# Batch 0's values as ten half loads, with a new order of all steps, in an attention and mixing kernel

## The chip, the cores and the metric

The kernel runs on one core of one Trainium2 chip. The metric is the device time of one execution in microseconds (us). The core's engines are named as in the profile: PE (TensorE, the matrix products; PEld is its weight load), DVE (VectorE), ACT (ScalarE), POOL (GpSimd) and SP (SyncE, which here issues all DMAs). Each engine executes its own instructions in order.

## The reference

Batch 8, 8 heads, 576 positions, head size 64. For each batch and head two attentions are added:

```
out_up    = repeat4( softmax(scale * q_d k_d^T) v_d )           # q_d, k_d, v_d: means of 4 positions
out_local = softmax(scale * q k^T where |i - j| < 4) v          # a band of 7 positions
x = out_up + out_local                                          # then to (8, 576, 512)
theta = x @ w_theta
y = w_tok_r @ (x * cos(theta)) + w_tok_i @ (x * sin(theta))     # over the 576 positions
u = x + y
out = u + max(u @ w_ch, 0)
```

All inputs and the output are float32; the products run in bfloat16.

## The kernel before, in words

**The work of a batch.** It is cut into small steps, each a Python function that issues a few instructions, and each named by two letters. A number behind the letters, as in mx 0.3, is the batch and the part.

- Loads: `lk` and `lq` bring k and q, one load of 288 KB for each pair of heads, four of each in a batch. `lv` and `lw` bring v in ten half loads of 128 KB, two for each of five chunks of positions. All land in 14 float32 buffers `st`.
- `ck`, `cq`, `cv` cast these to bfloat16, on DVE (v), ACT (a) or POOL (g). `tp` turns k and q on PE (nine 128x128 turns), `ev` evicts them into kT and qT. `kd` and `qd` form the sums of four positions.
- Local attention: `ps` (scores of one of three units), `ex` (exp on ACT), `mk` (mask, on DVE or POOL), `po` (product with v, five chunks), `nm` (normalise, two DVE instructions).
- Attention of the means: `pv` and `vd` (means of v), `sd` (scores), `ed` (exp), `nd` (product), `xn` (normalise), `xd` and `xc` (turn and evict).
- `xt` turns the local part and `xa` adds both into xT. Then `th` (theta), `cs` (cos and sin on ACT), `xm` (turn x back), `zz` (x times cos and sin, into z). The last 64 positions go through `tt`, `ct`, `zt` and, in batches 0 to 3, `zp` and `zc`; in batches 4 to 7 a transposing DMA, `dz`.
- Mixing over positions: `mx`, eight groups of nine products a batch (line 610), each evicted by `ua` (line 615). Then `up` and `uc` (turn), `ch` (product with w_ch), `rl` (max and add), `st` (store). The last 64 positions of two batches go together through `ht` and `rt`.

**Weights.** `la`/`ca` bring w_theta, `lc`/`cc` bring w_ch. `lb` loads w_tok_r and w_tok_i in nine pieces, `cb` casts them, `wp` turns them on PE and `wc` evicts them into WT. The first `mx` needs all of WT and all of batch 0's z.

**What sets the order.** `ORDER` is a string of some 1,200 words, one a step: two letters, and then the engine, the PSUM bank or the `st` buffer. The steps are issued in exactly that order, and the function `pin` chains all instructions of an engine, so each engine's order is the string's. `wm` issues products of a zero tile (line 715) that nothing reads: place and count, `wm0k` is 20 of them. `te` and `ts` load ACT's table for exp and for sin (line 720).

**Batch 0's v.** For the batches in `VT` v comes in another way than by `lv` and `lw`: `l1` loads it like k and q (four loads of 288 KB), `c1` casts, `t1` turns on PE, `e1` evicts on ACT, and `x1` turns it again into the five chunks, from where `cv` evicts it into v_w.

Of the kernel before, what the change touches and what calls it, by code (L numbers as in the profile page):

```python
# [55 lines left out]
l10 l11 c1g c1g k0 l12 lk3 l14 ckg c1v lk5 wm0k t101 c1g e1a kcg wm24 t123 e1a lq6 wm45 x12 cva ckg x13 cva x10 cvv
cqg lq7 lk8 lk9 tp45 cqg kcg kcg x12 lqa eva lqb kdg cvv kca cka wm62 tp67 lkc x13 lkd cvv eva ckv wm13 pv01 cqv lq0
la2 cqg lb1 tp45 qdv eva wm22 tp23 eva wm65 ps67 kdg vdv lq3 qdv ckg cka ps45 cag ex wm25 sd23 ex lb4 ed cbg lk5 sd01  # L60
cqg ps67 mkv ed po45 nm po23 nd45 nd01 la6 nm la7 xn xn lk8 mkg tp23 cag po45 ex xt6 po01 cqa eva la9 lqa mkg caa xd7
lqb ckg xca ckg nm tp23 nm xt4 xt5 lbd cag lbc cbg lb2 xt7 xa cqg lb1 eva lb0 cbg lb3 lb6 tp01 xa po23 th4 xa xm5 xa
lv7 cqg nm cbg th6 lw xt7 cbg th2 lv5 xm3 evv cbg ts cs tp01 lv8 lv9 cs cbg xa tt4 zz cs xm5 wp6 wp2 zz lw lw wp3 lw
lv4 lw cbg lqa zz ct lqd eva qdg ztv wp7 cba th4 wcv zp5 lkb xm6 wcv lkc kdg wcv wp2 wp3 wcv zcv wp0 wcv wp1 cs wp7
wca wcv ps45 lk2 lk1 wcv wcv ps23 te ex qdg ps01 lq0 zz kdv cva ex mx7 mx6 mx4 cvg ua sd23 cvg cvg mkv lc3 ex po01 ua
sd67 ed ed mkv mx5 ua nm po23 ua po01 cvg pv67 nm nm mkg vda mx4 ua po23 lq6 cqg po67 nd01 nm nd45 mx2 up3 xn lq7 ckg
xn cqg lk5 cka nm tp01 xd4 lk8 up5 uca eva xcv xt3 ucv lk9 tp67 cka xt4 xt0 ua ckg xt1 kdg lv4 xa xa xa mx5 xa eva lva
tp23 ua th4 xt0 lw xa evv cqg th5 xm1 lvb lcd lqc tt0 lw lk1 lv2 lv0 lw ts cs lw xm4 cqg cs tp67 ckg cqg th2 xm3 th5
ct lw cka zz tp01 cs qdg zz cs xm2 evv ztg lc6 lc5 zp4 mx6 ccg zz qdg zcv zz eva cvg mx7 ps45 te ex ua ps23 ua ckg kdv
ex mkv ps01 mx6 lq7 mx7 po45 sd23 ex lq8 lk3 kdg ed cvg sd01 cqg ckg ua lk4 lq9 mx6 tp23 mkv lva lw lvc lw nm ua tp45  # L70
up7 cvg mkv cvv ed mx0 eva cvg pv23 ccg ua ucv eva po67 po45 ua nm up1 nm vda ccg ccg ch0 nd67 lq1 xn nd23 lkb cqg cqa
tp45 uca qdg xn mx1 xd2 xt3 eva ps67 rl lq0 ua po45 xcv kdg qdg ps01 ch2 xa ckg ex mkg nm rl mx3 ps67 cqg lv2 cka po45
ex ua sd01 lkd xt2 ckg ex nm mx3 xt4 xt5 xa up2 ua cqa cqg tp67 cvv ed up3 xa evv uca th0 xa lv6 xt1 up2 xa lw th4 xm6
ucv ts cs uca th5 cvg lq5 ckg po01 cvg zz cs nm po23 xm7 cs ch6 nm tt4 tp01 lw ct tp23 th5 rl mkg ch4 lq7 zz st eva
evv rl po67 sd01 cs cqg cvg ztg po23 ch5 nm nm rl ch4 lv8 lw te ed cvg st pv67 vda zp0 zca lk4 cka lk3 lk1 tp23 cqa
mkg ckg lq9 lqb rl qdg lva lw xm1 eva ckg utg lv0 zz lw xm5 ch4 nd67 lvc zz xn lw nd01 mx5 lvd xn mx6 st ps23 rl lv2
# [25 lines left out]
def kernel(  # L102
# [290 lines left out]
    def cv(b, c, w):  # L393
        if b in VT:
            COPY[w](out=v_w[b % 2][:, c, :, 0:D], in_=at.pop(("x1", b, c)).rearrange("p (h d) -> p h d", d=D))
            return
        COPY[w](out=v_w[b % 2][:, c, :, 0:D], in_=at["v", b, c].rearrange("p (h d) -> p h d", d=D))  # L397
# [360 lines left out]
```

## Time and profile before

| | us |
|---|---|
| median of 3 runs | 236.6 (235.68 to 238.39) |
| the profiled execution | 236.41 |
| its span, first to last instruction | 234.7 |
| PE busy | 223.5 (95%) |
| DVE busy | 187.6 (80%) |
| ACT busy | 159.7 (68%) |
| POOL busy | 143.9 (61%) |

The span lies inside the execution's own time, 1.7 us less. An engine's busy time counts its computing instructions alone. PE's busy time includes the products of the zero tile, and PE's matrix products overlap one another, so a busy PE is not PE at its peak.

### The profile page before, as it was taken

The numbers are of one execution on the slowest core, as the hardware profiler recorded it, in microseconds if no ns is written. First come the engines' busy times: TensorE is split into PE (matmuls) and PEld (weight loads), VectorE is DVE, ScalarE is ACT, GpSimd is POOL, SyncE is SP. The second block draws the span as 40 slices with busy tenths as digits, with TensorE's granted clock in tenths as the row PEclk, the third lists the DMA queues.
The fourth block names the chain that finished last, engine by engine and source line by source line (L and its number), as shares of the span: only waits on it lengthen the run. The fifth ranks groups of instructions, "written<-read, shape, count | busy, mean of one in ns | idle before, by whom it ended". The sixth has DMA issues, their size and how long they took to land.

```text
span 234.7 us, 8524 instructions
## 1 busy us (share of the span) xinstructions
PE 223.5 (95%) x3500; PEld 155.7 (66%) x3500; DVE 187.6 (80%) x377; ACT 159.7 (68%) x239; POOL 143.9 (61%) x190
## 2 busy tenths in 40 slices
PE   7998899999999699999999999899999999999992
PEld 3555767687787466786688757676676665577740
DVE  5169997999898689888799869969898879466472
ACT  2389898669987779869987796859889358510000
POOL 7858999809999995983874628794598310100000
PEclk9999999999999999999999999999999999999998
DMA  6999979996959999999986206996967357674477
GB/s 196 383 392 386 287 163 276 391 244 143 290 162 250 243 345 212 224 224 244 287 183 173 61 0 141 292 236 139 127 155 169 73 124 197 91 221 109 110 226 244
DMA packets 76647, 49.35 MB, mean 210 GB/s; under 512 B 61120, under 2 KB 61120, under 8 KB 76608
## 3 DMA queue, kind: packets, MB, share of 16 engines
q1 hardware_dynamic: 76608, 48.81, 81.4%
q8 instruction: 27, 0.44, 0.8%
q14 instruction: 12, 0.10, 0.2%
HBM read 33.98 MB, written 9.44 MB: 185 GB/s over the span
## 4 chain that ended last, share of the span: by engine, by line
PE 85%; DVE 8%; issue 3%; DMA 2%; ACT 1%; SPq 0%; DVEq 0%
PE PS L610 29%; PE PS L635 12%; PE PS L548 10%; PE PS L304 5%; PE PS L531 3%; PE PS L512 3%; PE PS L715 3%; PE PS L587 2%; PE PS L483 2%; DMA z<-zT 2%; PE PS L275 2%; DVE tmp L521 2%; PE PS L448 2%; PE PS L624 2%; PE PS L652 1%
## 5 line engine op out<-in xcount | busy, mean ns | idle before, releaser
L610 PE MATMUL PS<-WT,z 128*128 128x288 bf16 x576 | 77.9, 286 | 0.4 <-DMA z<-zT 0.4
L610 PEld LDWEIGHTS <-z 128*128 128x128 bf16 x576 | 54.3, 98 | 16.0 <-DMA z<-zT 0.7
L615 DVE TENSOR_TENSOR uT<-PS,xT 128x288 bf16<-128x288 f32 x64 | 28.8, 452 | 12.4 <-PE PS L610 11.9
L548 PE MATMUL PS<-wth,xT 128*128 128x512 bf16 x128 | 32.2, 379 | 0.0
L635 PE MATMUL PS<-wch,uT 128*128 128x512 bf16 x128 | 31.1, 379 | 0.0
L569 POOL TENSOR_TENSOR zT<-xT,cst 128x512 bf16<-128x512 bf16 x7 | 8.1, 1153 | 35.9 <-ACT cst L566 27.6
L521 DVE TENSOR_TENSOR tmp<-PS,rl 128x512 bf16<-128x512 f32 x40 | 27.6, 691 | 1.4
L502 POOL TENSOR_TENSOR pm<-pm,band 128x1024 bf16<-128x1024 bf16 (+1 forms) x14 | 25.1, 1792 | 5.5 <-ACT pm L491 5.5
L537 DVE TENSOR_TENSOR xT<-PS,xdT 128x464 bf16<-128x464 f32 (+1 forms) x40 | 24.0, 628 | 4.5 <-PE PS L531 2.3
L640 DVE SCALAR_TENSOR_TENSOR osb<-PS,ur 128x512 f32<-128x512 f32 x32 | 21.8, 684 | 5.2 <-PE PS L635 4.9
L491 ACT ACTIVATE pm<-PS 128x1024 bf16<-128x1024 f32 (+1 forms) x24 | 20.4, 880 | 6.4 <-PE PS L483 6.4
L553 ACT ACTIVATE cs<-PS,pihc 128x512 bf16<-128x512 f32 x32 | 22.1, 692 | 3.0 <-PE PS L548 2.8
L331 POOL TENSOR_TENSOR two<-kT 128x580 f32<-128x580 bf16 x13 | 15.0, 1154 | 9.4 <-ACT kT L317 6.6
L720 ACT ACT_TABLE_LOAD x15 | 19.2, 1283 | 0.3
L635 PEld LDWEIGHTS <-uT 128*128 128x128 bf16 x128 | 11.9, 98 | 11.1
L554 ACT ACTIVATE cs<-PS 128x512 bf16<-128x512 f32 x32 | 19.2, 600 | 0.0
L594 DVE TENSOR_TENSOR z<-PS,cs 128x1024 bf16<-128x1024 bf16 x24 | 16.0, 681 | 2.4 <-PE PS L587 2.1
L548 PEld LDWEIGHTS <-xT 128*128 128x128 bf16 x128 | 11.2, 98 | 9.8 <-DVE xT L537 0.4
L438 ACT ACTIVATE pd<-PS 128x864 bf16<-128x864 f32 x16 | 13.8, 888 | 5.6 <-PE PS L427 5.6
L331 POOL TENSOR_TENSOR two<-qT 128x576 f32<-128x576 bf16 x13 | 14.9, 1148 | 4.3 <-ACT qT L317 4.0
L397 POOL CAST v_w<-st 128x512 bf16<-128x512 f32 x26 | 16.2, 647 | 0.0
L531 PE MATMUL PS<-ident,tmp 128*128 128x116 bf16 (+1 forms) x160 | 13.9, 215 | 2.1 <-issue 2.0
(116 smaller groups left out, 435.8 us busy)
## 6 DMA issues: line engine op xcount, KB each, us to landing
st<-in_k_dram SPq DMA_DIRECT2D x32, 288.0 KB, 5.3
st<-in_q_dram SPq DMA_DIRECT2D x32, 288.0 KB, 5.9
st<-in_v_dram SPq DMA_DIRECT2D x70, 128.0 KB, 5.0
out_dram<-osb SPq DMA_DIRECT2D x32, 256.0 KB, 3.0
st<-in_v_dram SPq DMA_DIRECT2D x4, 288.0 KB, 3.4
st<-in_moe_w_tok_r_dram SPq DMA_DIRECT2D x4, 288.0 KB, 6.3
st<-in_moe_w_tok_i_dram SPq DMA_DIRECT2D x4, 288.0 KB, 6.1
st<-in_moe_w_theta_dram SPq DMA_DIRECT2D x4, 256.0 KB, 7.2
```

What stands on the lines that cost most here:

```text
L331: nc.gpsimd.tensor_tensor(out=t, in0=src[:, :, 0:2], in1=src[:, :, 2:4], op=ALU.add)
L491: nc.scalar.activation(out=pm[(3 * b + u) % NPM][:, :, 0:n].rearrange("p e c j w -> p e (c j w)"), in_=at.pop(("ps", b, u))[:, :, 0:4 * W ...
L502: EW[w].tensor_tensor(out=t, in0=t, in1=m, op=ALU.mult)
L521: nc.vector.tensor_tensor(out=tmp[(NCH * b + c) % NTMP].rearrange("p g (j d) -> p g j d", d=D), in0=ps[:, :, :, 0:D], in1=r.unsqueeze(3).t ...
L531: nc.tensor.matmul(out=ps[:, kk::2, STEP * g:STEP * g + OWN[n]], lhsT=t[:, g, P * kk:P * kk + P], rhs=identw[:, :, lo:lo + OWN[n]], start= ...
L537: nc.vector.tensor_tensor(out=xT[b % 2][:, :, CH * c:CH * c + cnt].rearrange("p e (m j) -> p e m j", j=4), in0=at.pop(("xt", b, c))[:, :, ...
L548: nc.tensor.matmul(out=ps, lhsT=xT[b % 2][:, dc, P * c:P * c + P], rhs=wth[:, dc, :], start=(dc == 0), stop=(dc == 3))
L553: nc.scalar.activation(out=t[:, 0, :], in_=ps, func=AF.Sin, bias=pihc, scale=1.0)
L610: nc.tensor.matmul(out=ps, lhsT=z[b % 2][:, j, P * dc:P * dc + P], rhs=WT[:, j, cols], start=(j == 0), stop=(j == 8))
L615: nc.vector.tensor_tensor(out=uT[b % 2][:, dc, cols], in0=at.pop(("mx", b, i)), in1=xT[b % 2][:, dc, cols], op=ALU.add)
L635: nc.tensor.matmul(out=ps, lhsT=uT[b % 2][:, dc, P * c:P * c + P], rhs=wch[:, dc, :], start=(dc == 0), stop=(dc == 3))
L640: nc.vector.scalar_tensor_tensor(out=o, in0=at.pop(("ch", b, c)), scalar=0.0, in1=ur[b % 2][:, c, :], op0=ALU.max, op1=ALU.add)
```

## The change

`VT` is empty, so batch 0's v comes by `lv` and `lw` like that of the other batches; `l1`, `c1`, `t1`, `e1` and `x1` issue nothing. All words of `ORDER` are new in their order, and in many the engine, bank or buffer is another. No function is changed.

```
-VT = (0,)
+VT = ()
...
 ORDER = """
-l10 l11 c1g c1g k0 l12 lk3 l14 ckg c1v lk5 wm0k t101 c1g e1a kcg wm24 t123 e1a lq6 wm45 x12 cva ckg x13 cva x10 cvv
...
+lq0 lk1 lk2 lq3 cka ckv lq4 cqg wm0m tp01 cqv lk5 lk6 k0 wm24 tp23 ckv eva lq7 cqv lv8 lv9 lw ckv cqg lw lva lw lvb
...
 """
```

Of the zero-tile products there were 46 in eight places, now 67 in eleven. `te` and `ts` stood 15 times, now 17.

**SP at the start of the program.** Before, its first eight loads are v (line 367), k and q (line 288) of batch 0:

```order
L367 DMA st0_127<-in_v_dram 128x576
L367 DMA st1_128<-in_v_dram 128x576
L367 DMA st2_129<-in_v_dram 128x576
L288 DMA st3_130<-in_k_dram 128x576
L367 DMA st4_131<-in_v_dram 128x576
L288 DMA st5_132<-in_k_dram 128x576
L288 DMA st6_133<-in_q_dram 128x576
L288 DMA st7_134<-in_q_dram 128x576
```

In the changed kernel the first eight are all of batch 0's q and k. From the eighth on it reads:

```order
L288 DMA st7_134<-in_q_dram 128x576
L349 DMA st8_135<-in_v_dram 64x8x64
L349 DMA st9_136<-in_v_dram 64x8x64
L349 DMA st8_135<-in_v_dram 64x8x64
L349 DMA st9_136<-in_v_dram 64x8x64
L349 DMA st10_137<-in_v_dram 64x8x64 x2
L349 DMA st11_138<-in_v_dram 64x8x64 x2
L349 DMA st12_139<-in_v_dram 64x8x64
L288 DMA st13_140<-in_k_dram 128x576
L349 DMA st12_139<-in_v_dram 64x8x64
L288 DMA st1_128<-in_k_dram 128x576
L259 DMA st0_127<-in_moe_w_tok_r_dram 128x576
```

The v loads moved from the front of the queue behind batch 0's k and q, and are ten (line 349) where they were four.

**DVE between batch 0's last addition into xT and the first mixing.** Before, line 537 is `xa` 0.4, line 594 `zz`, line 569 `zt`, line 279 `wc`, line 582 `zc`:

```order
L537 TENSOR_TENSOR xT0_101<-PS_61,xdT0_99 128x4x112
L594 TENSOR_TENSOR z0_103<-PS_61,cs0_105 128x1024
L594 TENSOR_TENSOR z0_103<-PS_61,cs1_106 128x1024
L594 TENSOR_TENSOR z0_103<-PS_61,cs2_107 128x1024
L569 TENSOR_TENSOR zT_111<-xT0_101,cst_109 128x512
L279 COPY WT_126<-PS_61 128x576 x4
L582 COPY z0_103<-PS_61 128x512
L279 COPY WT_126<-PS_61 128x576 x4
L594 TENSOR_TENSOR z0_103<-PS_61,cs3_108 128x1024
```

And in the changed kernel, with line 323 a `kd` of batch 1:

```order
L537 TENSOR_TENSOR xT0_101<-PS_61,xdT0_99 128x4x112
L279 COPY WT_126<-PS_61 128x576
L323 TENSOR_REDUCE kd1_67<-kT1_63 128x2x5x29
L279 COPY WT_126<-PS_61 128x576
L594 TENSOR_TENSOR z0_103<-PS_61,cs0_105 128x1024
L569 TENSOR_TENSOR zT_111<-xT0_101,cst_109 128x512
L594 TENSOR_TENSOR z0_103<-PS_61,cs1_106 128x1024
L279 COPY WT_126<-PS_61 128x576 x5
L594 TENSOR_TENSOR z0_103<-PS_61,cs2_107 128x1024
L594 TENSOR_TENSOR z0_103<-PS_61,cs3_108 128x1024
```

One `kd` came in ahead of the products into z, and `zc` left DVE for ACT.

**ACT in the thetas of batches 4 and 5.** Lines 553 and 554 are cos and sin of one chunk, 565 and 566 those of the last 64 positions. Before, batch 5's first pairs have an eviction and the last positions between them:

```order
L720 ACT_TABLE_LOAD
L720 ACTIVATE idle_143<-pihc_142 128x1
L553 ACTIVATE cs0_105<-PS_61,pihc_142 128x512
L554 ACTIVATE cs0_105<-PS_61 128x512
L314 COPY qT1_65<-st11_138 128x1152
L553 ACTIVATE cs1_106<-PS_61,pihc_142 128x512
L554 ACTIVATE cs1_106<-PS_61 128x512
L565 ACTIVATE cst_109<-PS_61,pihc_142 128x4x64
L566 ACTIVATE cst_109<-PS_61 128x4x64
```

In the changed kernel the last of batch 4 and all four of batch 5 follow one another, behind a table load that comes after the exp of batch 6:

```order
L720 ACT_TABLE_LOAD
L720 ACTIVATE idle_143<-pihc_142 128x1
L553 ACTIVATE cs3_108<-PS_61,pihc_142 128x512
L554 ACTIVATE cs3_108<-PS_61 128x512
L553 ACTIVATE cs0_105<-PS_61,pihc_142 128x512
L554 ACTIVATE cs0_105<-PS_61 128x512
L553 ACTIVATE cs1_106<-PS_61,pihc_142 128x512
L554 ACTIVATE cs1_106<-PS_61 128x512
L553 ACTIVATE cs2_107<-PS_61,pihc_142 128x512
L554 ACTIVATE cs2_107<-PS_61 128x512
L553 ACTIVATE cs3_108<-PS_61,pihc_142 128x512
L554 ACTIVATE cs3_108<-PS_61 128x512
```

Five pairs of cos and sin now stand in a row on ACT at this place, where there were single ones.

More of the change, by code (lines that the diff above doesn't have):

```diff
@@ L51 @@
 QKD = (7,)
-VT = (0,)
+VT = ()
 ORDER = """
[L58 to L76, printed above, removed]
@@ new lines @@
+kdv wp3 tt1 th2 cbg wcv eva cbg ct wp6 wp1 zz xm4 ztv zz wcv lq7 lq2 lv4 lv8 cs xm3 wca lv9 wm53 wp7 cs lkb lw cqg zp5
+cqg zca cka wcv lka lqc wp4 lw qdg wcv wp0 wcv wp2 wp1 wcv xm5 wca tp67 eva zz lvd zz kdg tp01 eva lw mx4 ckg lv0 mx5
+ps23 ua lw mx4 lw ps67 lk5 lk1 ua te ex lq6 qdv mkg ua sd01 sd23 cvg cqa lq3 mx5 ed mx4 cvv ex ua ua cka po01 po67 ed
+nm cqa lv7 lkb wm51 ps45 tp23 ex nm lc2 lc8 lc4 mkg cvv cvg lca lkc lw lqd lv9 tp01 cvg eva ckg eva ckg up4 ucv mx5
+up4 mkv pv67 vda ua lq0 lw po23 cqg cqg lv5 nm po01 lw mx5 nm uca nd23 tp67 nd01 ua eva xn tp45 po23 xt6 kdg eva xn nm
@@ new lines @@
+xt7 ccg xd0 lk1 qdg ccg xca xt1 xa ps45 ps23 lv6 xa xa cka ckg mx0 xt6 ex ex lv3 ccv kdg ccv ua xt7 cvg xa th4 ts cs
+th5 cs up1 xm0 tp23 lw xa th6 th7 mkv lq2 lkb evv zz tt4 ch5 lq4 cs mkv xm0 lw lk8 zz rl xm6 lqa cs cqg ct lvc lk7 cqg
+tp23 xm7 zz ucv up0 ch4 qdg uca ch5 ztg zz eva rl zp6 ckg zcv cvg lvd cvg rl cqg mx7 lq0 sd01 lw po23 cvg nm te ed
+ps45 ua ex mx6 lq1 po01 sd23 ckg ua kdg cqa nm po45 mx7 ed tp01 lw nm mx6 po23 ua cvv pv45 eva tp01 mkg qdg ua lk9 mx7
+vda ckg nm kdv eva cqa cka lq5 ua nd23 nd45 lk2 mx0 cqa ps67 qdg xn lv6 ex xn ckg ua po23 ps45 lw utg lvb lv4 lw nm
@@ new lines @@
+cva ex ckg mkv ch1 cvg cqg rl sd67 ed xd0 mx2 sd45 ed xcv po01 xt3 ua cqa up2 lw nm ucv st tp67 up4 cvg lq3 cvg lk8
+tp01 mx2 lva eva cvg xt5 ucv xa tp67 eva xt3 ua lv7 xa xa xt2 tp01 eva up4 xt3 up5 kdg lk0 xa lw ucv po67 ucv eva lkc
+xm2 xa nm ps45 qdv ps01 ex tt3 pv45 mkv cqg ch6 rl ex th7 vda nd01 ts ct nd45 lv9 xn xn ckg cs ztg th6 lw cs th3 mkv
+po01 po45 ch7 lk2 kdg lw lqd xd6 zz nm th2 xm0 st rl ckg cs xca lq1 lq5 cqg nm xt1 xt3 zz xa lk6 zp7 tp45 cs xm6 zz xa
+xt2 zca eva xm0 lkb ch1 zz po67 nm ps45 te ex mx3 xa xt0 lv4 lw th6 xt2 lq3 lq8 ckg ckg tp45 mkg lv0 ts cs lw lvd lw
@@ new lines @@
+ua xm3 xa lkc st rl cqg th7 th0 cs xm1 cqg xa xm2 tt6 evv cvv ckg cs cvg zz tp45 zz qdg kdv mx3 ua mkv tp01 mx7 mx3
+lv2 eva eva lk1 ps45 ps01 cqg ct ua zz ckg cvv qdg ua cvv lv5 lw lv6 lw lw te ex utg po67 mx2 nm ex tp45 mx3 ua ztv
+sd01 eva ua cvg sd67 cqa ed po45 mx2 lv7 mkg ed pv01 nm ps45 po67 nm vda ex kdg kdg mx3 ckg ua nd01 nd67 th2 cvg lqa
+ua xn up3 lk3 ts cs xn xm0 st xt1 dt utg lvb ckv tp45 xd6 ch7 zz xca xa zp2 up6 uca zca mx0 mx1 ucv qdg po23 mkg rl
+ps67 eva ua sd45 ua te ed xt0 mx1 nm po23 mkg lw lw xa ex nm lq0 cvg sd45 po67 cva mx0 cvg cqa nm ht2 ua st lv9 po67
@@ new lines @@
+ed cva ua pv45 tp01 xt3 rt lk4 cqg vda mx2 lv8 nm lw evv xa lqc nd67 qdg lqd ua ch4 nd01 st xn tp23 xn cka up5 eva ucv
+cqa up6 uca rl mx7 ua lq1 mx5 ps01 ckg st po23 po67 nm lv2 mx4 ss xt2 ua ex xt3 cqa th5 lv6 qdg xt0 ua xa xa lw mkv
+xd1 th4 xt2 xm3 ts cs st sr nm lk0 zz th5 cs xca xa lw cs up6 xa up7 dk5 ch3 tt4 ch5 rl st dka uca kdg ucv rl ct th6
+sd01 lq7 te ed sd23 cka cvv ed po45 nm cqg lw ch7 xt0 lk4 rl xm1 ztg th4 xt5 xm7 lv3 dz cvg zz cva cvg ts cs xm1 up2
+xa xt0 utg dt ch3 cs xa xa ch5 rl st th0 rl st st cvg xm3 th6 th5 zz evg mkg cs ckg xm0 lvc dkd zz cs mx1 cs mx4 zz zz
@@ new lines @@
+ucv ua st evg po67 ps23 ua ps01 cqg te ex ch5 tt4 dk1 mx2 ex mx3 rl nm po01 lvb ua lw mkg po67 ua ts ct nm pv45 xt2
+mx3 up0 mx1 nm mx6 ua xm3 ztg ucv qdg vda ua xm7 ua nd45 xn dz nd01 mkg eva evg xn lw kdg mx6 zz ch4 lw xd5 st xca zz
+rl mx3 po01 lv9 ps45 ua cvg ua ps67 lw st lv2 te ex ex nm xa mx3 qdg kdg cvv xt0 mkg mx1 ua po45 sd67 xa sd23 du ed
+mx0 du ua nm xt1 mx4 xa ps67 ed ua cvv po23 po01 ex ch5 ht6 st xt7 lw nm ua mx4 cvg cvg xa mkg xt7 rt utv xa pv23 mkv
+th6 vda du du ua ch7 nd23 du rl ch4 nm ch5 ts cs nd01 xn tt6 rl dx dx ct rl mx4 ss po23 dx rl xn dx po67 po01 mx5 nm
@@ L98 @@
+nm th2 xt3 sr xd6 nm xt7 th0 th1 cs ua du xca ua xa ztg xt6 xa ch2 xa th3 zz du xt7 dz xt6 utg cs ht0 xa ch7 zz du rl
+th4 st st dt xa cs rl zz st st zz dx th1 st tt2 ch5 dx dx mx6 ct cs cs cs rl th7 ch5 cs rl rt dx zz mx4 mx5 mx7 mx1
+mx0 mx2 ss ztg zz zz ua ua zz sr mx3 dz ua ua ua mx6 st ua mx7 mx1 ua mx0 st ua ua ua mx6 ua mx1 ua mx0 ua ua mx1 ua
+st ch0 ch7 du ch6 ua ch1 ch2 du du utv du rl rl rl ch0 ch3 du du du utg du st rl rl st rl rl dt st st st st ch2 rl st
+ht1 st rt ss sr
 """
```

26 lines of the change are left out of this document (5 added, 21 removed).

## The prediction

> **What bounds the kernel now.** I read the page first, its shares and the clock row of its 40 slices:
>
> ```profile
> PE 223.5 (95%) x3500; PEld 155.7 (66%) x3500; DVE 187.6 (80%) x377; ACT 159.7 (68%) x239; POOL 143.9 (61%) x190
> ...
> PEclk9999999999999999999999999999999999999998
> ```
>
> PE is the busy one, and its clock is full throughout. Part of its start, though, is products of the zero tile, which only fill time. So I split the span at the first mixing, in the chain and in the view by stretches (PE's busy time is the second figure of a row):
>
> ```profile
> 28.64 0.50 PE PS L304 x9
> 29.39 0.99 PE PS L548 x4
> 30.61 0.86 PE PS L548 x4
> ...
> 40.62 3.41 PE PS L610 x27
> ...
> 63.47 0.80 PE PS L483 x80
> ...
> 229.35 0.88 PE PS L652 x4
> ```
>
> ```profile
> 0.00:40.62 40.62, 37.46 (x607) 23.89 (x608) 29.23 (x70) 29.09 (x41) 34.21 (x65) 1.00 0.93 297
> 40.62:230.25 189.63, 186.07 (x2894) 131.86 (x2894) 157.65 (x307) 130.62 (x199) 109.71 (x126) 1.00 0.81 192
> ```
>
> From the first mixing (40.62) to the last product (230.23) PE is busy 186.07 of 189.63 us. That stretch is bound by PE, and there a removed us of PE work is a us gained. Its holes are 3.56 us, most of it here (timeline of PE, idle time in brackets):
>
> ```profile
> 81.64 0.23 PE L531 MATMUL PS<-ident,tmp 128*128 128x116 bf16 x1 [2.02 <-issue]
> ...
> 151.70 0.32 PE L512 MATMUL PS<-v_w,pm 64*64 64x65 bf16 x16 [0.94 <-DVE tmp L521]
> ...
> 202.16 0.30 PE L610 MATMUL PS<-WT,z 128*128 128x288 bf16 x1 [0.41 <-DMA z<-zT]
> ```
>
> The start is a chain through several engines, with fillers in its gaps. PE is dense from about the first theta, at 29.39. The sum is therefore: when does the changed kernel reach its first theta, and what has PE still to do from there.
>
> **The turns that go cost PE nothing now.** Batch 0's v by turns, in the chain:
>
> ```profile
> 4.00 4.77 PE PS L715 x20
> 8.77 0.50 PE PS L378 x9
> ...
> 10.67 1.13 ACT xT L381
> 11.84 0.86 PE PS L390 x24
> ```
>
> `t1` is two times 0.50, `x1` is 40 products at 0.86/24, 1.4 us: 2.4 us of PE in all. They lie among zero-tile products, which go on until about 21. What they do cost is order: with them v comes first, and the keys of the local scores after it, so that the first exp stands at 20.05:
>
> ```profile
> 20.05 1.94 ACT L491 ACTIVATE pm<-PS 128x1024 bf16<-128x1024 f32 x2
> 22.06 1.67 ACT L438 ACTIVATE pd<-PS 128x864 bf16<-128x864 f32 x2
> ...
> 23.06 2.12 POOL L502 TENSOR_TENSOR pm<-pm,band 128x1024 bf16<-128x1024 bf16 x1
> ```
>
> **The new start, step by step.** In the changed kernel the first eight loads are q and k, of the same size and in the same places of the queue as the eight before; the eighth was issued at 4.05 and took 6.2 us (the maximum of these two):
>
> ```profile
> L288 SPq DMA_DIRECT2D st<-in_q_dram x2: 432/432/432, 3.6 to 4.1; - x2
> ...
> DMA to landing us min/median/max: 5.9/6.1/6.2
> ```
>
> So the last q is there at 10.3, 0.75 behind the one before it (390 GB/s). PE has its 6 and 22 zero-tile products (two more than where the row at 4.00 ends, 0.215 each, a quarter of the 0.86 of the theta at 30.61, which has four products of that width): 9.2. Then a turn of nine (0.50 by the row at 28.64), 4 fillers, turn, 11 fillers, two turns: 14.4. The eviction of the last and the scores behind it:
>
> ```profile
> L317 ACT COPY kT<-PS 128x1152 bf16<-128x1152 bf16 x10 | 11.2, 1122 | 2.2 <-PE PS L304 2.2
> ...
> L397 POOL CAST v_w<-st 128x512 bf16<-128x512 f32 x26 | 16.2, 647 | 0.0
> L413 ACT CAST vd<-PS 128x512 bf16<-128x512 f32 x5 | 2.9, 586 | 3.8 <-PE PS L405 3.5
> L416 ACT CAST vd<-PS 32x256 bf16<-32x256 f32 x10 | 3.6, 360 | 0.1
> ```
>
> Eviction 0.2 + 1.12: 15.8. Scores 0.5: exp of unit 0 from 16.3, 3.7 us sooner than before. But ACT then holds exp, a cast of v (0.6) and exp of unit 1, 0.97 each by the two in 1.94: 18.9. POOL masks unit 1 in 2.12: 21.0. Behind it POOL casts v's fifth chunk, 0.65: 21.65. `pv`, six products, under 0.5: 22.1. ACT has meanwhile finished the third exp, two casts, small copies and both `ed` (1.67 by the row at 22.06): 22.7; `vd` is 0.59 + 2 x 0.36: 24.0. From here it goes as before, where the timeline has:
>
> ```profile
> 24.05 0.43 PE L448 MATMUL PS<-vd,pd 128*72 128x65 bf16 x8 [0.73 <-DVE tmp L521]
> ...
> 25.07 0.66 PE L304 MATMUL PS<-ident,k_tm 128*128 128x128 bf16 x9
> ```
>
> ```profile
> 25.83 0.69 DVE L459 TENSOR_TENSOR xdn<-PS,rd 72x512 bf16<-72x512 f32 x1
> ...
> 28.12 2.27 DVE L537 TENSOR_TENSOR xT<-PS,xdT 128x464 bf16<-128x464 f32 x4
> ```
>
> Two `nd` in 1.02: 25.0, as before (25.07). Second `xn` to 26.2, `xd` and `xc` 0.9: 27.1, and DVE adds into xT from 27.15 where it was 28.12. So **the exps' lead of 3.7 us shrinks to about 1 us**, since what feeds the means, the fifth chunk and `vd`, is late next. And PE has in its queue ahead of the first theta: three `xt` until 27.3 (the last waits for `nm` at 27.05), turn 0.50, `po` 0.38, 3 fillers 0.65, turn 0.50: **29.35, against 29.39**. The last cast of w_theta on ACT (behind `xc`, three casts, 0.6 to 0.7 each) is done at 29.0, so it doesn't change this. Bounds: 28.3, when the second addition is done and nothing else holds; 31, if each of some fifteen hand-overs slips by 0.1. I take 29.4, the same as before.
>
> **v's ten halves.** They are issued behind the eighth load. Rows of such loads (timeline, group and stretch):
>
> ```profile
> 27.44 7.93 SPq L349 DMA_DIRECT2D st<-in_v_dram  x10
> ...
> L349 SPq DMA_DIRECT2D st<-in_v_dram x70: 595/612/1724, 27.4 to 178.3; - x70
> ...
> 30.00:35.00 5.00, 5.00 (x65) 3.54 (x63) 4.97 (x9) 4.97 (x11) 5.00 (x8) 1.00 0.71 153
> ```
>
> 0.61 us each, or 0.79 as these ten went; 153 GB/s where the start has 390. Landing from 10.3, with one k load (0.75) between: the tenth at 17.2 (at 0.79: 19.0). It is used at 21.0, behind the mask on POOL; that mask is the cover. The bound: above (21.0 - 10.3 - 0.75) / 10 = 1.0 us for each half the end comes later by ten times the excess. Ends: 0.33 (a half at the start's rate) gives nothing, 1.72 (the longest) gives 7 us. I take 0.61, the median of 70. Since ten went at 0.79, and one took 1.72, late halves are a rival below. Weights come behind them: the last piece of w_tok_i by about 30, before POOL reaches it.
>
> The Trainium skill, "DMA: Bandwidth & Descriptors", section "Why small descriptors are slow (HBM only)", speaks against these loads: a 256-byte piece pays about 3 bus cycles on 8. By it alone a half would take, as an estimate, 0.33 x 11/8 = 0.46 us, and the sum would stay as it is; the trace, with 0.61 to 0.79, shows more than the rule asks.
>
> **What remains from the first theta on.** Before, PE had by then done three turns of batch 1; the changed kernel has done two: +0.50. It keeps 3 fillers ahead of `wp` and 1 in batch 1: 4 x 0.215 = +0.86. All else is the same number of products. DVE to the first mixing, from 27.15: four additions 2.27, `ev` 1.35, `nm` 0.9, a cast 0.6, an addition 0.6, two `wc`, `kd`, two `zz` and `zt` 4.4, five `wc` 2.25, two `zz` 1.36: 13.7, less 0.07 overlap at each of 20 seams, so 39.5; with 0.4 of waits 39.9:
>
> ```profile
> L317 DVE COPY kT<-PS 128x1152 bf16<-128x1152 bf16 x4 | 5.4, 1345 | 0.0
> ...
> L323 DVE TENSOR_REDUCE kd<-kT 128x290 bf16<-128x1160 bf16 x3 | 4.1, 1352 | 0.0
> ...
> L594 DVE TENSOR_TENSOR z<-PS,cs 128x1024 bf16<-128x1024 bf16 x24 | 16.0, 681 | 2.4 <-PE PS L587 2.1
> ...
> L279 DVE COPY WT<-PS 128x576 bf16<-128x576 bf16 x8 | 3.3, 450 | 1.2 <-PE PS L275 1.2
> ```
>
> PE gets there at 40.62 + 0.50 + 0.65 - 0.80 = 41.0, since batch 1's scores (80 products, 0.80) now come behind the first mixing. So PE covers the `kd` that came ahead of `zz`, by 1.1; without that cover it costs 1.35. The removed 2.4 us give nothing, as said. At the end both orders run `mx` 6.1 to 7.7, `ch` and `ht` back to back; `dz` of batch 6 is now issued some 16 us ahead of its use, so its hole of 0.41 can go. I leave the holes at 3.56: the 2.02 has no cause that the trace shows.
>
> **Sum.** 234.7 + 0 (first theta) + 0.50 + 0.86 = 236.1 us of span; plus 1.7 around it (236.41 - 234.7): 237.8. The profiled execution lies 0.2 below the median, so **237.9 us**, 0.5% above 236.6.
>
> **Rivals.**
> - *Slower: ACT in batches 4 and 5.* The order has five cos and sin pairs in a row, and two table loads shortly before. Rows:
>
> ```profile
> L553 ACT ACTIVATE cs<-PS,pihc 128x512 bf16<-128x512 f32 x32 | 22.1, 692 | 3.0 <-PE PS L548 2.8
> ...
> L720 ACT ACT_TABLE_LOAD x15 | 19.2, 1283 | 0.3
> ...
> L554 ACT ACTIVATE cs<-PS 128x512 bf16<-128x512 f32 x32 | 19.2, 600 | 0.0
> ```
>
> From `mx` 3.7 to `cs` 5.3 ACT has eight pairs (10.3), three table loads with their dummies (4.5), two `ed`, one `ex`, and seven casts and evictions: 21.6, less 0.08 at 26 seams, 19.5. PE has in that time eight thetas, five `ch`, seven `xt`, small turns (16.0), and 3.1 more before it needs `cs` 5.3's bank: 19.1. From an ACT that is behind by nothing the excess is 0.4, and every us that it enters behind is a us of waiting. So it decides from an ACT that enters level with PE. For it: over the whole span ACT is busy 68%, here it has more work than PE. Against: in the stretch ahead, from `mx` 3.2 to 3.7, its steps sum to about 7 against PE's 13, so it can come in early. Two us behind give about 2.5: **240.4**.
> - *Slower: v's halves late.* At 1.3 us each, 3.0 later: **240.9**.
> - *Faster: the holes go.* The 2.02 and the 0.41 don't come back and the theta starts at 28.3: 237.9 - 2.4 - 1.1 = **234.4**; with the other 1.1 of holes gone, 233.3.
>
> **How the numbers follow.** Within 1% (234.2 to 239.0; less a measurement of this kernel can't tell from no change): the forecast 0.46, with the weaker part of the faster rival 0.04: 0.50. ACT or another eviction behind 0.27, v late 0.12: slower 0.39. Faster, the strong part of its rival: 0.11. The range goes from 234.2, leaving out the strong faster cases, to 241.5, which takes in both slower rivals with 0.6 more; beyond it I leave 0.09.
>
> **What would show it.** First exp near 16.3, second `xn` near 26, first theta near 29.4, first mixing near 41, PE's holes behind it near 3.6. Wrong if the fifth `cv` on POOL waits for a v load (then halves are the cause), if PE has a hole at `ch` 3.2 or `ps` 6.1 (ACT), or if the first theta is off by over 1.5 us, in either direction.

## The result, and the profile after

The changed kernel takes **237.78 us** (median of 20 runs, 236.05 to 242.6); the kernel before, run beside it, 236.47 (20 runs, 234.05 to 239.42). The ratio is 1.009, with a 95% interval of 1.0061 to 1.0118: slower by 0.6 to 1.2%. The ratio leaves out executions more than 1.5% above the fastest of their kernel, and so it is not the ratio of the two medians, which is 1.0055. The prediction was 237.9. The execution that was profiled took 237.02, with a span of 235.3.

The page of the changed kernel, the same two lines as before:

```profile
PE 224.8 (96%) x3436; PEld 156.7 (67%) x3463; DVE 186.7 (79%) x380; ACT 161.1 (68%) x252; POOL 138.3 (59%) x174
...
PEclk9998899999999999999999999999999999999998
```

PE is still the busy engine. New is the 8 in the fourth and fifth slice of the clock, which was 9 throughout before (a slice is 5.9 us, so this is somewhere in 17.6 to 29.4). The view by stretches finds it (PE's busy time is the second figure, the clock the third from the end):

```profile
18.30:21.70 3.40, 1.93 (x80) 1.29 (x79) 2.53 (x5) 3.36 (x8) 2.87 (x2) 1.00 0.89 303
21.70:25.10 3.40, 2.97 (x21) 1.66 (x18) 1.88 (x6) 2.22 (x5) 1.08 (x2) 0.51 1.01 352
```

For 3.4 us PE runs at half its clock, behind a stretch of the same length in which it was busy only 1.93 us. The timeline of PE over that place, with idle time in brackets (L715 are the fillers, L448 and L453 are `nd`):

```profile
19.21 0.45 PE L512 MATMUL PS<-v_w,pm 64*64 64x65 bf16 x32
20.89 0.32 PE L512 MATMUL PS<-v_w,pm 64*64 64x65 bf16 x16 [1.23 <-POOL pm L502]
21.45 0.40 PE L405 MATMUL PS<-v_w,pu 128*32 128x512 bf16 x4 [0.24 <-ACT pd L438]
21.67 0.35 PE L408 MATMUL PS<-v_w,pu 128*32 128x256 bf16 x2
22.23 0.59 PE L715 MATMUL PS<-warm 128*128 128x512 bf16 x1 [0.21 <-ACT pd L438]
23.04 1.49 PE L715 MATMUL PS<-warm 128*128 128x512 bf16 x3 [0.22 <-issue]
24.32 0.68 PE L448 MATMUL PS<-vd,pd 128*72 128x65 bf16 x8
...
30.02 0.67 PE L304 MATMUL PS<-ident,q_tm 128*128 128x128 bf16 x9
30.74 2.54 PE L548 MATMUL PS<-wth,xT 128*128 128x512 bf16 x11
...
42.10 2.37 PE L610 MATMUL PS<-WT,z 128*128 128x288 bf16 x18
```

The third `po` waits 1.23 us for the mask of unit 1 on POOL. The fillers then take 0.4 to 0.5 each instead of 0.215, and they stand ahead of `nd`, whose `vd` was ready at 23.26 (the end of its last cast in ACT's timeline). The first theta comes at 30.74, where 29.4 was predicted and 29.39 was before; the first mixing at 42.10, where 41.0 was predicted and 40.6 was before.

The stretch behind it went the other way. From the first mixing on (the last product ends at 230.49):

```profile
42.10:231.00 188.90, 186.45 (x2957) 133.23 (x2975) 156.36 (x306) 135.17 (x210) 114.81 (x127) 1.00 0.86 196
```

PE is busy 186.45 of 188.39 us up to its last product, so its holes are 1.9 us where before had 3.56. No gap is longer than 0.23. (The records of some 18 products are missing from this row, so the holes are rather fewer than 1.9.) In these two executions the late start (1.5) and the missing holes (1.6) almost cancel.

### The profile page after: what moved, and what is told of

The parts are those of the page before. It is cut to its first block, busy times and chain, and to the rows that moved or that the text cites. A ratio compares the mean times of both kernels' runs of the same rounds, so it can differ in the third digit from the quotient of the medians.

```text
span 235.3 us, 8416 instructions
## 1 busy us (share of the span) xinstructions
PE 224.8 (96%) x3436; PEld 156.7 (67%) x3463; DVE 186.7 (79%) x380; ACT 161.1 (68%) x252; POOL 138.3 (59%) x174
## 4 chain that ended last, share of the span: by engine, by line
PE 82%; ACT 4%; issue 4%; DMA 3%; DVE 2%; POOL 2%; SPq 1%; POOLq 0%; DVEq 0%; ACTq 0%
PE PS L610 27%; PE PS L548 10%; PE PS L635 10%; PE PS L715 6%; PE PS L304 6%; PE PS L531 3%; PE PS L512 3%; PE PS L483 2%; PE PS L587 2%; DMA st<-in_v_dram 2%; PE PS L448 2%; PE PS L275 2%; PE PS L453 2%; PE PS L560 1%; PE PS L624 1%
## 5 line engine op out<-in xcount | busy, mean ns | idle before, releaser
L615 DVE TENSOR_TENSOR uT<-PS,xT 128x288 bf16<-128x288 f32 x64 | 27.7, 451 | 10.4 <-PE PS L610 10.1
L548 PE MATMUL PS<-wth,xT 128*128 128x512 bf16 x121 | 31.0, 379 | 0.4
L635 PE MATMUL PS<-wch,uT 128*128 128x512 bf16 x115 | 29.9, 379 | 0.9 <-issue 0.3
L537 DVE TENSOR_TENSOR xT<-PS,xdT 128x464 bf16<-128x464 f32 (+1 forms) x40 | 24.1, 630 | 4.3 <-ACT xdT L471 2.1
L502 POOL TENSOR_TENSOR pm<-pm,band 128x1024 bf16<-128x1024 bf16 (+1 forms) x13 | 24.6, 1897 | 4.7 <-ACT pm L491 4.7
L569 POOL TENSOR_TENSOR zT<-xT,cst 128x512 bf16<-128x512 bf16 x6 | 7.6, 1265 | 23.9 <-ACT cst L566 23.9
L331 POOL TENSOR_TENSOR two<-qT 128x576 f32<-128x576 bf16 x14 | 16.8, 1201 | 7.0 <-ACT qT L317 7.0
L554 ACT ACTIVATE cs<-PS 128x512 bf16<-128x512 f32 x32 | 19.7, 614 | 0.0
L297 POOL CAST q_tm<-st 128x576 bf16<-128x576 f32 x20 | 13.1, 664 | 10.0 <-DMA st<-in_q_dram 8.8
L317 ACT COPY qT<-PS 128x1152 bf16<-128x1152 bf16 x13 | 14.6, 1124 | 5.3 <-PE PS L304 5.2
L715 PE MATMUL PS<-warm 128*128 128x512 bf16 x62 | 16.7, 404 | 0.7 <-issue 0.4
L397 POOL CAST v_w<-st 128x512 bf16<-128x512 f32 x24 | 15.8, 671 | 1.2 <-DMA st<-in_v_dram 1.2
```

What stands on the lines that cost most here:

```text
L502: EW[w].tensor_tensor(out=t, in0=t, in1=m, op=ALU.mult)
L537: nc.vector.tensor_tensor(out=xT[b % 2][:, :, CH * c:CH * c + cnt].rearrange("p e (m j) -> p e m j", j=4), in0=at.pop(("xt", b, c))[:, :, ...
L548: nc.tensor.matmul(out=ps, lhsT=xT[b % 2][:, dc, P * c:P * c + P], rhs=wth[:, dc, :], start=(dc == 0), stop=(dc == 3))
L615: nc.vector.tensor_tensor(out=uT[b % 2][:, dc, cols], in0=at.pop(("mx", b, i)), in1=xT[b % 2][:, dc, cols], op=ALU.add)
L635: nc.tensor.matmul(out=ps, lhsT=uT[b % 2][:, dc, P * c:P * c + P], rhs=wch[:, dc, :], start=(dc == 0), stop=(dc == 3))
L715: nc.tensor.matmul(out=bank(place[0]), lhsT=warm[:, 0:P], rhs=warm, start=True, stop=True)
```

## The experiments

Each run gave a time and one profile. Three points of each profile's timeline are set side by side here (us): first exp on ACT, first theta and first mixing on PE, and the end of the last product.

| run | first exp | exp to theta | theta to mixing | mixing to last product | time, median | ratio to before, 95% |
|---|---|---|---|---|---|---|
| before | 20.05 | 9.30 | 11.20 | 189.67 | 236.47 | 1 |
| e0, before again | 20.48 | 9.52 | 10.98 | 188.07 | 235.25 (one) | none |
| changed | 16.05 | 14.69 | 11.36 | 188.39 | 237.78 | 1.0061 to 1.0118 |
| e1, narrow fillers in three places | 16.64 | 14.85 | 11.55 | 188.39 | 238.3 | 1.0073 to 1.0184 |
| e2, no fillers ahead of `nd` | 17.21 | 13.76 | 11.55 | 189.47 | 238.0 | 1.004 to 1.0111 |
| e3, 2048-byte rows | 15.90 | 14.61 | 11.34 | 189.70 | 237.81 | 1.0047 to 1.0166 |
| e4, narrow fillers, bank 4 | 15.81 | 13.29 | 11.34 | 189.63 | 236.44 | 0.9983 to 1.0061 |
| e5b, masks exchanged | 15.99 | 14.66 | 11.33 | 192.14 | 239.07 | 1.0074 to 1.0198 |
| e6, four fillers fewer | 16.03 | 14.68 | 11.54 | 189.50 | 237.97 | 1.0028 to 1.0117 |
| e7, halves, old order | 23.81 | 9.03 | 10.97 | 188.40 | 239.0 | 1.0086 to 1.0206 |
| e8, the same, fifth chunk apart | 21.50 | 9.73 | 10.97 | 192.17 | 239.85 | 1.0082 to 1.02 |
| e9, e4 and less DVE and fillers | 17.18 | 13.56 | 10.72 | 188.82 | 236.6 | 0.9992 to 1.0049 |
| e10, e9 and masks, v casts | 16.65 | 12.78 | 10.72 | 190.50 | 237.17 | 1.0021 to 1.0071 |

Two things move by themselves from one execution to the next: the first exp (15.8 to 17.2 in kernels whose order up to there is the same) and the last stretch (before itself has 189.67 and 188.07). The two middle columns move less: 14.61 to 14.69 from exp to theta in the four kernels that have the same steps there (changed, e3, e5b but for its masks, e6), and 0.2 in either column for the kernel before. So the reasons are read from them, and differences of 0.2 are not.

**e0: the kernel before, a second profile.** No edit.

> The kernel before, unchanged, for a second profile of it. Its first profile had PE idle 3.56 us between the first mixing and the last product, 2.02 of it in one hole at 79.6 that no wait explains. Theory 'the hole belongs to the order': it comes again, near 2 us at the same product (line 531). Rival 'the hole is this execution's': PE idle there is 1.0 to 2.0 us and the span about 2 us shorter, 232.5 to 233.5. The first theta at 29.4 and the granted clock 1.00 in 20 to 25 us in both.

The 2.02 hole of the first profile did not return, and the span is 233.5, 1.2 shorter, where the rival said about 2. Of the holes behind the first mixing these are there again:

```profile
150.08 0.32 PE L512 MATMUL PS<-v_w,pm 64*64 64x65 bf16 x16 [0.94 <-DVE tmp L521]
...
200.99 0.30 PE L610 MATMUL PS<-WT,z 128*128 128x288 bf16 x1 [0.38 <-DMA z<-zT]
```

So the 0.94 and the 0.4 belong to the old order, and the 2.02 to one execution.

**e1 and e2: the clock, and the fillers ahead of `nd`.** In e1 narrow products of the zero tile stand in three places, those of the last in the place of the five fillers ahead of `nd`; in e2 these five are taken out. Rows of SP, PE and the other engines are from each run's timeline, as above.

```diff
e1
-po45 mkv po23 cvg
+po45 wn4b mkv po23 wn23 cvg
-vda la5 wm05 nd01
+vda la5 wn2d nd01
+        if kind == "wn":
+            for _ in range(int(place[1:], 36)):
+                nc.tensor.matmul(out=bank(place[0])[:, 264:512], lhsT=warm[:, 0:P], rhs=warm[:, 0:248], start=True, stop=True)
e2
-vda la5 wm05 nd01
+vda la5 nd01
```

> The changed kernel, with narrow zero-tile products (248 columns, in the idle half of a bank) where PE waits: 11 ahead of the third po, 3 behind it, and 13 in place of the five wide ones ahead of nd. No other work is changed. Theory 'clock': PE's idle time from 19.7 to 22.2 lets the granted clock fall to a half from about 21.7 to 25.1, and this makes the start late; kept busy, the clock stays at 1.00 in 20 to 25 us, nd starts near 23.4 (24.3 now), the first theta near 29.2 (30.7 now) and the time is 1.2 to 1.7 us below the changed kernel's 237.8: 236.1 to 236.6, a ratio of 0.998 to 1.001 to before. Rival 'loads': the start is late because v's halves and the weights behind them land late; fillers change nothing, 237.5 to 238.

> The changed kernel without the five zero-tile products ahead of batch 0's nd. Theory 'clock': the five ran at half clock and ended at 24.3 while vd was ready at 23.3, so nd starts 1.0 us earlier, but PE is idle for longer and the half clock lasts beyond 25; first theta 30.0 to 30.7, time 237.2 to 238. Rival 'the fillers are the delay' (the clock doesn't matter): first theta at 29.7, time 236.8.

In e1 the clock stayed at 1.00, but nothing was won, since the narrow products ahead of `nd` had a wait of their own (bank 2, behind `nm`), and `nd` started at 25.67:

```profile
24.30 1.54 PE L721 MATMUL PS<-warm 128*128 128x248 bf16 x13 [1.59 <-DVE tmp L521]
```

So e1 tells nothing on the clock's price. In e2 `nd` follows `vd` at once, and exp to theta is 13.76 instead of 14.69, although PE still ran at half clock from about 24.1 to 27.5: the fillers ahead of `nd` are part of the loss. The time (1.0075) does not show it, and the theta itself stands at 30.97, because the first exp of this execution came 1.16 later than in the changed kernel.

**e4: the clock alone.** Only the narrow products that wait for nothing; the five fillers ahead of `nd` stay.

```diff
-po45 mkv po23 cvg
+po45 wn4b mkv po23 cvg
```

> The changed kernel with eleven narrow products of the zero tile (bank 4, a half that nobody uses, so they wait for nothing) ahead of the third po; the five fillers ahead of nd stay. Theory (the start is one chain, and PE's time from the first theta on is fixed): the granted clock stays at 1.00 over 21 to 25 us, the fillers ahead of nd end when vd is ready, nd starts near 23.5 where it was 24.3, first theta and the end 0.8 to 1.1 sooner: about 236.8. Rival (what the start gains is given back by the first mixing, where DVE or ACT is as late as PE): clock 1.00, but the first mixing stays within 0.3 of 42.1 and the time near 237.8.

```profile
19.35 1.34 PE L721 MATMUL PS<-warm 128*128 128x248 bf16 x11
20.66 0.32 PE L512 MATMUL PS<-v_w,pm 64*64 64x65 bf16 x16
...
21.99 1.24 PE L715 MATMUL PS<-warm 128*128 128x512 bf16 x4 [0.27 <-ACT pd L438]
23.07 0.44 PE L448 MATMUL PS<-vd,pd 128*72 128x65 bf16 x8
...
29.10 2.54 PE L548 MATMUL PS<-wth,xT 128*128 128x512 bf16 x11
...
40.44 2.37 PE L610 MATMUL PS<-WT,z 128*128 128x288 bf16 x18
```

```profile
20.00:25.00 5.00, 4.44 (x79) 3.13 (x78) 4.43 (x12) 3.69 (x7) 2.58 (x4) 1.00 1.04 384
```

With eleven products whose result nobody reads the clock stays at 1.00, `nd` starts at 23.07 instead of 24.32, the theta comes 13.29 behind the exp instead of 14.69, and the first mixing at 40.44. Theta to mixing stays at 11.34, so nothing is given back. The ratio falls from 1.009 to 1.0022 (0.9983 to 1.0061); the two intervals only touch. By these figures the lost clock and the slow fillers behind it are the greater part of what the change cost. What is left can't be told from no change.

Each execution's mean granted clock is on record as well, and it bears this out beyond the profiled ones. A loss of 3.4 us at half clock takes 0.007 off the mean of 235 us; the clock also falls behind the last product (to 0.50 at 234 to 236 in the changed kernel), so a mean of 0.995 is not yet such a loss. The changed kernel has 0.982 to 0.993 in 19 of its 20 executions. The twentieth has 0.998, and at 236.05 it is the fastest. e6, which leaves the same gap in PE's start, has 0.975 to 0.993 in nine of ten; the tenth has 1.000 and takes 234.81, against a median of 237.97. The kernel before, run beside the experiments, has 0.995 or more in 51 of 52, and e4 in all ten. Two executions are few, but they are faster by 1.7 and 3.2 than the medians of their kernels with no edit at all. A full clock alone is no gain: e1 has 0.995 to 1.000 and takes 238.3, for the wait that it brought in.

**e5 and e5b: the mask on POOL.** The masks of units 1 and 2 of batch 0 are exchanged between DVE and POOL.

```diff
-cva lk1 ed mkg wm21 po23 nm lb0 lb2 po45 mkv po23
+cva lk1 ed mkv wm21 po23 nm lb0 lb2 po45 mkg po23
```

> The changed kernel with the masks of units 1 and 2 of batch 0 exchanged: unit 1 on DVE, unit 2 on POOL. Theory (the mask on POOL is what the third po waits for, 1.23 us, and that idle time also costs the clock): the third po starts near 20 instead of 20.9, clock 1.00 over 21 to 25, nd near 23.5, first theta 0.8 to 1.1 sooner, about 236.8. Rival (the same gap comes from DVE's nm, or from ed and vd on ACT, which are as late): the third po starts sooner, but nd stays near 24.3 and the time near 237.8.

> The changed kernel with the masks of units 1 and 2 exchanged, again, since the first profile of it can't be read. Theory (the mask on POOL is the gap's cause): third po at 20.6 or sooner, behind nm, clock mostly 1.00, nd near 23.5, time 236.5 to 237. Rival (with the mask gone, nm on DVE, as late by 0.3 us only, holds the third po, and PE still idles enough to lose its clock): third po at 20.5 to 20.7, clock 0.5 over 22 to 25, time near 237.8.

e5 took 238.1 (ratio 1.003 to 1.0174); its profiled execution had a span of 571.2 us, with the mixing's products at 570 ns (286 in the changed kernel), so nothing is read from it. In e5b:

```profile
20.51 0.32 PE L512 MATMUL PS<-v_w,pm 64*64 64x65 bf16 x16 [0.91 <-DVE tmp L521]
...
22.98 1.48 PE L715 MATMUL PS<-warm 128*128 128x512 bf16 x3 [0.22 <-issue]
24.26 0.68 PE L448 MATMUL PS<-vd,pd 128*72 128x65 bf16 x8
```

The rival holds, though the time, 239.07, is above its 237.8 (this profile also has four holes of 0.5 to 1.0 behind the first mixing). The third `po` comes 0.38 sooner, and then waits for `nm`, which has to free its bank. PE is idle almost as long, the clock is 0.50 over 22 to 25 again, and exp to theta is 14.66. The mask was only the last of several waits at that place.

**e3: the size of v's pieces.** Batch 0's v is read in runs of 2048 bytes; the rows that it takes are other ones than the reference's.

```diff
+        if b == 0:
+            nc.sync.dma_start(out=at["v", b, c][W * g:W * g + W],
+                              in_=v[b].rearrange("h (p r) d -> (h p) (r d)", r=8)[lo:lo + W])
+            return
```

> The changed kernel, but batch 0's ten half loads take 64 runs of 2048 bytes each, the same number of bytes from the same tensor, in place of 512 pieces of 256 bytes (so batch 0's v holds other rows than it should; the computation is the same in kind and amount). Theory 'clock': v's tenth half lands well before POOL casts it at 20.8 and PE waits for the mask, not for v, so the dip of the clock stays and the time is within 0.4 of 237.8. Rival 'loads': nine halves that were issued in 9.1 us go in about 3.5, all that is behind them lands 4 to 5 us sooner and the first theta comes 1 us or more sooner, 236.5 or below.

The halves on SP's queue, in the changed kernel and in e3:

```profile
4.58 9.12 SPq L349 DMA_DIRECT2D st<-in_v_dram  x9
```

```profile
4.75 8.54 SPq L350 DMA_DIRECT2D st<-in_v_dram  x9
```

1.01 us each, and 0.95 with the eight times longer runs. The halves in short runs take 0.85 to 1.01 over the profiles of the new order (0.85 in e2, 0.89 in e6), so 0.95 is no different from them. The size of a piece is not what they cost here, and the start is the same (14.61).

**e7 and e8: the halves without the new order.** The kernel before with ten half loads in the place of its four whole ones, and without `c1`, `t1`, `e1` and `x1`. In e7 a k load overwrites the fifth chunk of batch 0's v before its cast, so that chunk holds other values; e8 gives it a tile of its own.

```diff
-VT = (0,)
+VT = ()
-l10 l11 l12 l14
+lv0 lw lv1 lw lv2 lw lv4 lw lvd lw   (e7: lvc in the place of lvd)
-lkd cvv
+cvv lkd                              (e8 alone)
```

> The kernel before with one part of the change alone: v of batch 0 comes in ten half loads, in the place of its four whole loads, and its casts, turns and evictions go; all other steps stay in the old order. Theory (a half takes about 1.0 us of the queue, as measured behind the q and k loads): the ten take 10 us where the four took 3, q and k land up to 7 us later, the first exp is near 26, the time 241 to 243. Rival (a half costs 0.46 to 0.61 when the queue is empty): q and k 1.6 to 3.1 later, less what the removed turns free, the time 238 to 239.5. If the turns had been on the path, it would come out below 236.5.

> The kernel before with v of batch 0 as ten half loads in the place of the four whole ones, as in the run before it, but with the fifth chunk in a staging tile of its own, so that no k load comes between it and its cast (there DVE waited 7.2 us for that load). Theory (the old order can't use the freed turns: PE's start waits for the loads of q and k, which come 3.7 us later behind halves of 0.68 each than behind four whole loads): first exp near 23, the time 238 to 239. Rival (the late start in the run before came from the fifth cast alone): first exp near 20.5 to 21, the time 236 to 237.

The first exp of e7 is at 23.81, and its time 239.0: DVE waits 7.16 us for the k load ahead of the fifth cast. So e8 is the one to read; its queue:

```profile
0.80 4.14 SPq L348 DMA_DIRECT2D st<-in_v_dram  x6
...
5.67 2.67 SPq L348 DMA_DIRECT2D st<-in_v_dram  x4
...
10.95 0.91 SPq L287 DMA_DIRECT2D st<-in_q_dram  x2
```

Here, with less ahead of them in the queue, a half takes 0.68. In e8 the last q of batch 0 is issued by 11.9 (the last row) instead of 7.7, and the first exp is at 21.5, where before has 20.05 and 20.48: later by 1.0 to 1.5, less than the theory's 23, more than the rival's 21. The first mixing is at 42.2. The time is 1.4% above before, more than either theory.

But the loads are not all that differs. The halves leave PE idle at the start here too, and the clock is lost, in e7 from 19.8 to 23.2 and in e8 from 14.6 to 18.1 (the first row is PE's timeline, the second the view by stretches):

```profile
13.58 0.68 PE L303 MATMUL PS<-ident,k_tm 128*128 128x128 bf16 x9 [3.06 <-POOL k_tm L296]
...
14.65:18.05 3.40, 2.79 (x18) 1.38 (x18) 1.26 (x3) 2.83 (x5) 3.03 (x7) 0.50 1.03 399
```

In the profiled execution of e8 it is lost a second time, for 3.4 us from 154.6, behind holes of 0.94 and 1.23; these, another hole of 1.39 and the slow products are part of the 192.17 in the last stretch. Its four executions are slower the lower their mean clock is: 237.96 at 0.998, 238.98 at 0.993, 240.73 at 0.986, 241.27 at 0.979. So e8 shows that the halves in the old order are no gain, and it does not tell apart what the later loads cost, what the clock cost, and whether the 2.4 us of PE that the turns took came back in part.

**e6, e9 and e10: from the first theta to the first mixing.** e6 takes out the four fillers that the prediction counted as 0.86; e9 takes e4, leaves out the same four, and moves one `kd` of batch 1 from DVE to POOL; e10 is e9 with the masks exchanged, v's fourth chunk cast by POOL and the fifth ahead of the mask.

```diff
e6 (and e9)
-wm53   (ahead of wp7)
-wm51   (batch 1)
e9
-kdv wp3 tt1
+wp3 tt1
-wp4 lw qdg wcv
+wp4 lw qdg kdg wcv
e10
-cva lk1 ed mkg wm21 po23 nm lb0 lb2 po45 wn4b mkv po23 cvg ckv
+cvg lk1 ed mkv wm21 po23 nm lb0 lb2 po45 wn4b cvg mkg po23 ckv
```

> The changed kernel without the four fillers that the prediction counted behind the first theta (three ahead of wp, one in batch 1), 4 x 0.215 = 0.86 us of PE. Theory (PE-bound from the first theta on): 0.86 sooner, about 236.9. Rival (PE merely covers DVE's kd and zz ahead of the first mixing, or something else is as late): 0 to 0.2 sooner, and a gap of the same size appears on PE ahead of the first mixing.

> The kernel with the narrow products in bank 4, less the four fillers behind the first theta, and with the kd ahead of the first mixing (1.35 on DVE) moved to POOL behind qd. Theory (between the first theta and the first mixing DVE and PE are level, so only both together shorten it): first theta near 29.1, first mixing 0.6 to 0.8 sooner than 40.4 minus nothing else, the time 0.8 below the run with the narrow products alone: 235.5. Rival (something third, the casts of w_tok_i or POOL, is as late): first mixing 11.3 behind the first theta as now, the time 236.3.

> The same, and on top the mask of unit 1 on DVE and that of unit 2 on POOL, and the fourth chunk of v cast by POOL instead of ACT, the fifth ahead of the mask. Theory (vd on ACT is what nd waits for once the clock is full; ACT has 0.62 less ahead of it and POOL 2.1 less): nd 0.4 to 0.8 sooner, first theta 0.3 to 0.5 sooner, about 235.1. Rival (the tenth half lands only then, or nm on DVE is as late): nothing beyond the run before it, 235.5.

In e6 theta to mixing did not shrink (11.54); a gap came in the place of the fillers:

```profile
38.07 0.40 PE L579 MATMUL PS<-ident,zT 128*128 128x128 bf16 x4 [0.42 <-DVE zT L569]
38.67 2.41 PE L275 MATMUL PS<-ident,uT 128*128 128x128 bf16 x25 [0.20 <-DVE z L594]
```

By the rival this is what DVE's `kd` and `zz` cost once PE no longer covers them. But DVE's `zT` took 1.35 in this execution and 0.42 in the changed kernel (the rows are in the last section), and both gaps stand behind it. Without them e6 would have some 10.9 (11.54 less 0.62, an estimate), so this profile does not show that the fillers are free. In the changed kernel DVE waits for PE's turns there, by 0.40 in all, which gives the cover for `kd` and `zz` as an estimate:

```profile
38.39 0.46 DVE L279 COPY WT<-PS 128x576 bf16<-128x576 bf16 x1 [0.17 <-PE PS L275]
39.07 1.45 DVE L279 COPY WT<-PS 128x576 bf16<-128x576 bf16 x3 [0.23 <-PE PS L275]
```

In e9, with the 1.35 us of `kd` off DVE too, theta to mixing is 10.72, shorter than e4's by 0.62. The three fillers alone are 0.65, so how much `kd` has to do with it is not shown. e9's first theta, expected near 29.1, came at 30.74, since its first exp came at 17.18. e10 has the shortest way from exp to theta of the new order, 12.78. The expected 0.8 us is not seen in the times of e9 (1.002) against e4 (1.0022), whose intervals are wider than that; and e10 (1.0046) is no better than e9, though its start is. It lost again behind the mixing, to these and smaller ones:

```profile
57.79 0.52 PE L483 MATMUL PS<-qT,kT 64*64 64x64 bf16 x39 [1.02 <-issue]
...
183.33 1.26 PE L610 MATMUL PS<-WT,z 128*128 128x288 bf16 x9 [0.89 <-DVE uT L615]
```

No version that was run is shown to be faster than the kernel before.

## Why the prediction was right, and where it was not

The time and the range held (237.9, and 237.78 measured; 234.2 to 241.5). That the two agree to 0.1 is luck. The sum put the first theta where it was before, and added 1.36 of PE work behind it. The runs show the opposite weight: the theta came 1.3 late, for a reason that was not in the sum, and no run shows the added work as time. e4 keeps all of it, and is 0.5 above the kernel before, with an interval from 0.4 below to 1.4 above. In the profiled execution fewer holes then hid most of the late start.

- *First exp 16.3:* 16.05 in the profile, 15.8 to 17.2 over the runs. Right.
- *v's halves, 0.61 each:* mis-sized. They took 1.01, just at the bound of 1.0 that the prediction gave (0.85 to 1.01 over the profiles). The cover still held: the fifth `cv` had no wait for a load in the changed kernel, and e10, where POOL was free for it sooner, shows when the load is there: `cv` waits 0.74 us and starts at 19.49, against 21.0 as the prediction's time of use and 20.78 in the changed kernel. There the last half was issued 0.5 later than in e10, so about 0.8 of the cover was left, as an estimate.

```profile
19.49 0.66 POOL L397 CAST v_w<-st 128x512 bf16<-128x512 f32 x1 [0.74 <-DMA st<-in_v_dram]
```

- *The chain to `vd`:* mask done 20.84 (21.0), fifth `cv` 21.59 (21.65), `vd` 23.26 (24.0). That the exps' lead would be lost to `cv` and `vd` was right.
- *"Two `nd` in 1.02: 25.0", and the first theta at 29.4, "the same as before":* the step that failed. `nd` took 24.32 to 25.8, and the theta came at 30.74, 1.3 late. The prediction had PE at full clock, as in the trace of before, and fillers that cost nothing. It followed ACT, POOL and DVE through 19.7 to 23, but not PE, which has its third `po`, `pv` and the first fillers there, and nothing else that could run. e4 shows the price: with the clock kept, exp to theta is 13.29, where the prediction's own times give 13.1 (29.4 less 16.3). The bound of 31 did take the measured value in.
- *DVE to the first mixing covered by PE, by 1.1:* too large by the rows, which have DVE waiting for PE by 0.40 there, an estimate of the cover. In the changed kernel this cost nothing. e6 does not measure it, because of its long `zT`.
- *The removed turns give nothing:* not shown. In e8 they are gone and the time is not less, but it has later loads and lost clock as well.
- *Holes left at 3.56:* wrong by 1.6 for this execution. The 2.02 did not come back even in the kernel before (e0). The 0.41 of batch 6's `dz` went, as the prediction allowed, and so did the 0.94 behind `nm` near 151. New in the order is a hole of 0.87 to 0.93 at 183 to 187, behind `uT` on DVE, in four of the eight other profiles of it (e3, e5b, e6, e10).
- *Rivals:* no hole at `ch` 3.2 or `ps` 6.1, so ACT was in time there. The price of 0.3 at the very end (4.8 us from the last product to the last store, 4.5 before) was in no rival.

Against e0 the changed execution is later by 1.1 at the first mixing, by 0.3 behind it and by 0.4 at the end, 1.8 in all; against the first profile of before by 1.5, -1.3 and 0.3. The ratio of 1.009 is 2.1 us. The medians of the two kernels differ by 1.3. So the late start of 1.1 to 1.5 is more than half of the cost, and e4 gives back 1.3 of it by the medians, 1.6 by the ratios. How the rest is split between the added PE work and holes that differ between executions stays open.

## What to carry to other kernels

When an order is rewritten, list for each stretch of the start how long PE has nothing that may run, and not only which wait ends last: here about 1.5 us of idle time within 3.4 cost half the clock of the next 3.4, and whatever stood in the queue there, fillers too, was paid double. A filler must wait for nothing: the one in e1 that writes a bank still being read was an additional wait ahead of the critical product. And a hole in one profile is not a term of a sum before a second profile shows it again.
